# Score scale moved into the exponential, first pair's running sums added by small matmuls, row maxima written per head, and new engine, queue and order tables, in a fused attention and two-MLP kernel

## The chip, the cores and the metric

The kernel runs on one core of a Trainium2 chip. The metric is the device time of one execution in microseconds, the median over the runs; lower is better.

## The reference, cut to what matters

Three layers follow each other. The first is causal attention on 4 batches of 8 heads (32 heads, handled as 16 pairs) with 576 positions and head size 64, where each score gets a bias from running sums of `max(s, 0)`:

```python
scale = 1.0 / np.sqrt(D)
scores = scale * np.matmul(q, k.transpose(0, 1, 3, 2))
cum = np.cumsum(np.maximum(s, 0.0), axis=-1)
bias = -(cum[:, :, :, None] - cum[:, :, None, :])
scores = np.where(causal, -1000000000.0, scores + np.minimum(bias, 0.0))
attn = np.exp(scores - np.max(scores, axis=-1, keepdims=True))
attn = attn / (np.sum(attn, axis=-1, keepdims=True) + 1e-09)
out = np.matmul(attn, v)
```

The second layer is a gated MLP: `h = relu(x @ w_in)`, the second half of `h` is normalised over its features, mixed over positions by `w_spatial` (576 x 576) plus a bias, multiplied by the first half and projected by `w_out`. The third is `sigmoid(xr @ w_r) * (relu(xk @ w_k)**2 @ w_v)`, with `xk` and `xr` mixtures of a position and the one before. The MLP weights come in 64-bit floats.

## The kernel before, in words

**Tensors.** Every fp32 matrix product is made of fp32r matmuls on a high part and a low part of each operand, so a part is first copied ("high") and then subtracted ("low"). For a pair p of heads the tile `big` (three sets, set p % 3) holds four regions U, W, V, X. `st_T` (L347) fills them: `wh` and `xh` are the high parts of q and k, `ud` and `vd` copies of them on the other 64 partitions, `ul` and `vl` the low parts. A few of the first 64 rows of W and X are used as extra rows of the contraction: the three parts of the running sums (X rows 0 to 2, against ones in W) and the negated row maximum (W row 3).

**Stages of a pair.** `st_S` (L390) computes rough scores, high part by high part, in 12 units s0 to s11 (6 per head); each is one matmul (L397) into one of three PSUM buffers, and VectorE reduces it to row maxima (`jk`, L404). `fin` transposes the maxima (L416), ScalarE copies them (L418) and a DMA writes them into W row 3 (L419); one `fin` covers both heads, except for pair 0, which has one each (Ma, Mb). `st_E` (L431) computes the exact scores in units e0 to e9 with two matmuls per piece (L436), ScalarE takes the exponential (L457) and GpSimd zeroes above the diagonal (L461). `st_V` (L468) multiplies with v in blocks a0 to a4 and b0 to b4 (L480 to L484, plain fp32), `fa` and `fb` copy the result out (L494), and n1, n2, n2b, n30, n31 divide by the sums through two tiny DMAs and a broadcast DMA (`r`, `rd`, `rb`; L499, L506, L512, L516).

**Decoding.** In between, the weights are turned from 64-bit floats into high and low fp32r parts, in 64 jobs of 128 x 256: dL loads (L124), dF is two ScalarE instructions (L132, L133), dD three on VectorE and one on GpSimd (L138 to L145), dT a copy on ScalarE and a subtraction on GpSimd (L153, L154) into one of the buffers of `ring`, dS stores it (L158).

**Order.** The order of issue is written by hand, and each engine works in that order. `START` (L586) holds pair 0 and the first parts of pairs 1 and 2. `step(p)` for p = 1 to 14 runs, by the list `ORDER` (L527), the exact scores of pair p, the products with v of pair p-1, the rough scores of pair p+1 and the parts of pair p+2 (of which `vd` and `vl` come a step later). `TAIL1` and `TAIL2` (L857, L861) hold the end of attention, the fetch of the decoded weights WV and WU, the first products of the MLP (g0 to g4: 12 matmuls of 512 columns each; q0 to q7: 12 of 288), the statistics of g0 to g4 on VectorE and the preparation of `w_spatial` (p0 to p4). After them everything is ordered by loops. The table `ENGINE` (L111) says which engine makes a copy or subtraction, `QUEUE` (L114) which of the two hardware queues (SP or ScalarE's) issues a DMA.

**Pair 0.** The running sums of all heads are built in `aug` (32 partitions x 3 parts x 576, `sums`, `bases`, `sums2`, L315 to L327), which lies in set 2 of `big`. `rx00` and `rx01` (L330) are DMAs that put the rows of pair 0 into its X region; the first rough scores read them.

Of the kernel before, what the change touches and what calls it, by code (L numbers as in the profile page):

```python
# [25 lines left out]
def tile_kernel(  # L26
# [141 lines left out]
    def dec_part(nm):
        q, f, n = PARTS[nm]
        if len(q) <= (n if jobs else 0):  # L170
            return

        if nm == "dL" and len(loaded) + len(first) > 2:
            dec_part("dD" if first else "dF")
        if nm == "dF" and len(first) > 1:
            dec_part("dD")
        if nm == "dD" and len(second) > 1:
            dec_part("dT")
        if nm == "dT" and len(third) >= len(ring):
            dec_go("dS")  # L180
        if q:
            f(*q.pop(0))
# [122 lines left out]


# [40 lines left out]
    def st_T(p, pre="", heads=(slice(0, 2),)):  # L347
        g = p % G
        by = {"q": scale, "k": 1.0}

# [12 lines left out]
        def first(nm, i, eng):  # L363
            if eng == "S":
                nc.scalar.activation(out=hi(nm, i), in_=raw(nm, i), func=ACTF.Copy, scale=by[nm])
            else:
                (nc.gpsimd if eng == "P" else nc.vector).tensor_scalar(
                    out=hi(nm, i), in0=raw(nm, i), scalar1=by[nm], scalar2=1.0, op0=ALU.mult, op1=ALU.mult)

        def second(nm, i, eng):  # L370

            h = (hi if nm == "q" else dup)(nm, i).bitcast(F32)
            if eng == "P" and nm == "k":
                nc.gpsimd.tensor_tensor(out=lo(nm, i), in0=raw(nm, i), in1=h, op=ALU.subtract)
            else:
                nc.vector.scalar_tensor_tensor(  # L376
                    out=lo(nm, i), in0=raw(nm, i), scalar=by[nm], op0=ALU.mult, in1=h, op1=ALU.subtract)
# [12 lines left out]
    def st_S(p):  # L390
# [40 lines left out]
    def st_E(p):  # L431
# [154 lines left out]
    START = """cw0 ldk0 lds mask cx0 cx1 ldk1 sums bases sums2 ldq0 ldq1 0wh0 0wh1 0ul0 rx00 0ul1 rx01 augd 0xh1 dL dL  # L586
               pads1 0xh0 dL pads0 0ud0 s5 s0 0ud1 cw1 tiny s1 cw2 1wh1 ldq2 1wh0 s8 1ud0 s3 dF s10 dD 1ud1 dT lv1 s9
               0vd0 0vl0 cx2 s4 1rows dF 1ul1 s2 1ul0 Ma s6 ltv0 pads2 s7 1xh0 dS 1s0 2wh1 1xh1 1s4 dL dF 2wh0 dD dD
               1s10 s11 lv0 1s3 0vd1 e0 dT 0vl1 ldk2 1s6 e1 Mb 2ul0 2rows e3 2ud0 2xh1 2xh0 2ul1 1s2 1s1 1vd0 1vd1 ldq3
               2vd1 ldq4 1vl1 1s7 e2 e4 1s9 dS 1s8 2vl1 1s11 e5 e8 ones 1s5 e7 1M 1vl0 ldk3 2vd0 e9 2ud1 dL 2vl0 e6 dF"""  # L590
# [465 lines left out]
```

## Time and profile before

| | us |
|---|---|
| median of the runs (3) | 698.87 |
| lowest and highest run | 696.9, 701.27 |
| profiled execution, its own time | 697.19 |
| span of its profile, first to last instruction | 695.5 |

The profile is of one execution. Its span is cut into stretches in the rows below; each row of an engine's timeline has the start, the duration, the engine, the line, the operation, the tiles written and read, and in square brackets how long the engine had been idle and what ended that.

### The profile page before, as it was taken

Reading aid. Unit: us, or ns where it says so; the run is one execution under the profiler, and the core shown is the slowest. Engines: PE = TensorE matmul, PEld = TensorE weight load, DVE = VectorE, ACT = ScalarE, POOL = GpSimd, SP = SyncE. Lnnn points to the kernel's source line nnn. Section 1 sums busy time; section 2 is a strip of 40 time slices with the busy share of each in tenths; the row PEclk is TensorE's granted clock in tenths of the full one; section 3 lists DMA queues with packets and bytes.
Section 4 is the critical chain, followed back from the end, with each engine's and each line's share of the span. In section 5 each row is a group of like instructions: output and inputs, shape, how many; then the busy total and the mean of one; then the engine's idle time right before and its main releaser. Section 6 shows DMA issues by size and latency. Waiting matters only on the chain.

```text
span 695.5 us, 10926 instructions
## 1 busy us (share of the span) xinstructions
PE 655.0 (94%) x3657; PEld 562.8 (81%) x3657; DVE 520.1 (75%) x1053; ACT 357.5 (51%) x780; POOL 352.3 (51%) x497
## 2 busy tenths in 40 slices
PE   2699999999999859999999999999999999999998
PEld 1476766667767749999999999988989889898987
DVE  8969898989862487858868847269697786968763
ACT  4688888888763375565566453341323324133230
POOL 5655656665673346558458557242444444244330
PEclk9999999999999969999999999999999999999999
DMA  7455556564456626463254474440001010000101
GB/s 183 121 122 143 154 144 160 140 164 130 115 163 182 195 90 190 140 211 127 87 193 140 125 262 152 160 204 31 15 2 46 0 46 1 30 16 1 45 1 46
DMA packets 64880, 77.91 MB, mean 112 GB/s; under 512 B 28661, under 2 KB 45461, under 8 KB 64311
## 3 DMA queue, kind: packets, MB, share of 16 engines
q1 hardware_dynamic: 64433, 76.08, 36.6%
q10 hardware_dynamic: 390, 1.12, 0.6%
q8 instruction: 29, 0.48, 0.3%
q14 instruction: 28, 0.23, 0.1%
HBM read 54.05 MB, written 21.79 MB: 109 GB/s over the span
## 4 chain that ended last, share of the span: by engine, by line
PE 72%; DVE 13%; DMA 8%; ACT 2%; issue 2%; SPq 1%; POOL 1%; DVEq 0%; ACTq 0%; POOLq 0%
PE mm L682 54%; PE mm L767 7%; DVE jk L404 4%; PE ps L436 3%; DVE big L376 3%; DMA qk<-in_qk_dram 3%; PE pv L484 3%; PE s L397 2%; PE pv L481 1%; DMA d_wo<-hl 1%; DMA big<-d_wv 1%; DMA big<-mt 1%; DVE f L143 1%; DVE g L140 1%; DVE big L102 1%
## 5 line engine op out<-in xcount | busy, mean ns | idle before, releaser
L682 PE MATMUL mm<-big 128*128 128x384 f32 (+2 forms) x1176 | 203.4, 332 | 3.4 <-ACT vr L719 3.0
L682 PEld LDWEIGHTS mm<-big 128*128 128x128 f32 x1176 | 191.3, 188 | 12.9 <-ACT vr L719 3.4
L682 PE MATMUL mm<-w,vb 128*128 128x512 f32 (+1 forms) x304 | 90.4, 381 | 0.0
L965 DVE TENSOR_TENSOR r<-r 128x384 f32<-128x384 f32 x48 | 53.7, 1118 | 46.6 <-ACT r L962 46.6
L436 PE MATMUL ps<-big 128*128 128x288 f32 (+4 forms) x384 | 82.7, 334 | 4.3 <-DMA big<-mt 3.3
L397 PE MATMUL s<-big 128*128 128x288 f32 (+4 forms) x192 | 66.4, 416 | 16.9 <-DMA big<-big 12.3
L457 ACT ACTIVATE e<-ps 128x288 f32<-128x288 f32 (+3 forms) x160 | 64.0, 435 | 30.5 <-PE ps L436 28.5
L145 POOL TENSOR_TENSOR f<-f,raw 128x256 int32<-128x256 int32 x64 | 53.1, 829 | 45.6 <-DVE f L143 37.0
L397 PEld LDWEIGHTS s<-big 128*128 128x128 f32 x192 | 36.9, 205 | 46.2 <-DVE mx L404 21.8
L404 DVE CUSTOM_DVE_ANT_0 jk<-s,mask 64x64 bf16<-64x64 f32 (+4 forms) x160 | 64.4, 424 | 10.4 <-PE s L397 8.6
L436 PEld LDWEIGHTS ps<-big 128*128 128x128 f32 x384 | 60.7, 198 | 12.6 <-DMA big<-mt 4.6
L767 PE MATMUL mm<-ws,vb 128*128 128x288 f32 x384 | 60.5, 307 | 7.4 <-DVE ws L120 7.0
L682 PEld LDWEIGHTS mm<-w,vb 128*128 128x128 f32 x304 | 56.0, 188 | 11.2
L767 PEld LDWEIGHTS mm<-ws,vb 128*128 128x128 f32 x384 | 55.7, 197 | 8.8 <-DVE ws L120 8.1
L484 PE MATMUL pv<-e,vp 128*65 128x448 f32 (+2 forms) x192 | 62.6, 434 | 0.0
L120 POOL TENSOR_TENSOR hl<-f,hl 128x256 fp32r<-128x256 f32 x42 | 40.5, 965 | 42.5 <-ACT hl L105 42.3
L985 DVE RECIPROCAL rr<-rr 128x512 f32<-128x512 f32 x18 | 60.4, 3353 | 0.6
L461 POOL TENSOR_SCALAR_AFFINE_SELECT e<-e 128x128 f32<-128x128 f32 (+1 forms) x160 | 52.1, 357 | 14.9 <-ACT e L457 13.0
L966 ACT CAST vb<-r 128x384 fp32r<-128x384 f32 x48 | 24.6, 513 | 56.9 <-DVE r L965 56.9
L708 POOL TENSOR_TENSOR gh<-mix,vb 128x384 fp32r<-128x384 f32 x24 | 25.5, 1069 | 52.3 <-ACT vb L707 51.2
L682 PE MATMUL mm<-gh,wo 128*128 128x288 f32 x256 | 51.3, 294 | 0.0
L708 POOL TENSOR_TENSOR big<-mix,big 128x384 fp32r<-128x384 f32 x24 | 26.0, 1089 | 46.3 <-ACT big L707 37.6
(124 smaller groups left out, 1282.6 us busy)
## 6 DMA issues: line engine op xcount, KB each, us to landing
qk<-in_qk_dram SPq DMA_DIRECT2D x28, 288.0 KB
rb<-rd SPq DMA_DIRECT2D x16, 288.0 KB
out_dram<-rr SPq DMA_DIRECT2D x17, 256.0 KB
raw<-in_moe_w_in_dram SPq DMA_DIRECT2D x16, 256.0 KB
vp<-in_v_dram SPq DMA_DIRECT2D x16, 256.0 KB
raw<-in_moe_w_k_dram SPq DMA_DIRECT2D x16, 256.0 KB
raw<-in_moe_w_v_dram SPq DMA_DIRECT2D x16, 256.0 KB
big<-d_wk SPq DMA_DIRECT2D x8, 512.0 KB
```

The costliest lines, as they stand in the source:

```text
L145: nc.gpsimd.tensor_tensor(out=f, in0=f, in1=low, op=ALU.add)
L397: nc.tensor.matmul(out=ps[:, 0:kn], lhsT=W[g][:, h, 128 * i:128 * i + 128], rhs=X[g][:, h, k0:k0 + kn], start=True, stop=True,)
L404: nc.vector.tensor_tensor_reduce(out=jk[r0:128, 0:kn], in0=ps[r0:128, 0:kn], in1=mask[r0:128, m0:m0 + kn], scale=1.0, scalar=(dst if mid e ...
L436: nc.tensor.matmul(out=ps[:, o:o + b - a], lhsT=st[g][:, h, 128 * j:128 * j + 128], rhs=mv[g][:, h, 64 + a:64 + b], start=(n == 0), stop=( ...
L457: nc.scalar.activation(out=e[:, o:o + n], in_=ps[:, 0:n], func=ACTF.Exp)
L461: nc.gpsimd.affine_select(out=d, in_=d, pattern=[[1, w]], base=0, channel_multiplier=-1, compare_op=ALU.is_ge, fill=0.0,)
L484: nc.tensor.matmul(out=pv[0:VW, 1, 448 - w:448], lhsT=lt, rhs=e[:, OFF[j]:OFF[j] + w], start=False, stop=(j == 4),)
L682: nc.tensor.matmul(out=ps, lhsT=x, rhs=y, start=(m == 0), stop=(m == n - 1))
L708: nc.gpsimd.tensor_tensor(out=dst[1][:, kc, :], in0=t, in1=dst[0][:, kc, :].bitcast(F32), op=ALU.subtract)
L767: nc.tensor.matmul(out=o, lhsT=x[:, sc, dd], rhs=y[:, sc, t], start=(sc == 0 and m == 0), stop=False)
L965: nc.vector.tensor_tensor(out=r, in0=r, in1=r, op=ALU.mult)
L985: nc.vector.reciprocal(out=r, in_=r)
```

## The change

- The factor 1/8 on q goes: `wh` is a plain copy and `ul` a plain subtraction, so both can run on any engine. The running sums are multiplied by 8 instead (in the instruction that takes `max(s, 0)`), and the exponential gets `scale=1/8`.
- For pair 0 the rough scores no longer read the rows of the running sums in X: the contraction is over the 64 partitions of q and k alone, and three more matmuls per unit add the rows of `aug` through `pick`, a 32-row selection of a head (36 small matmuls in all).
- Ma and Mb, one per head, replace M for every pair.
- The rule by which a decode part first makes room moves from `dec_part` to `dec_go`.
- Two extra ring buffers are put in front of the ring instead of behind it, after TAIL1.
- `ENGINE`, `QUEUE`, `ORDER`, `START`, `TAIL1`, `TAIL2` are new. In the steps `ud` moves from ScalarE to GpSimd and `vd` from VectorE to ScalarE. For the last pairs the DMAs n13, d14, n15, d15 and b15 move from SP to ScalarE's queue.

```diff
+    pick = ec.tile([BH, 2, 128], F32R, name="pick")
...
+    def picks():
+        COPY[ENGINE["pk"]](pick, ident[0:BH, 0:2].rearrange("p (h o) -> p h o", o=1).broadcast_to([BH, 2, 128]))
...
-        nc.vector.tensor_scalar(out=srow, in0=srow, scalar1=0.0, scalar2=None, op0=ALU.max)
+        nc.vector.tensor_scalar(out=srow, in0=srow, scalar1=0.0, scalar2=1.0 / scale, op0=ALU.max, op1=ALU.mult)
...
+            COPY[eng](hi(nm, i), raw(nm, i))
...
+            subtract(eng, out=lo(nm, i), in0=raw(nm, i), in1=h)
...
+            lanes = slice(64, 128) if p == 0 else slice(0, 128)
             nc.tensor.matmul(
-                out=ps[:, 0:kn], lhsT=W[g][:, h, 128 * i:128 * i + 128], rhs=X[g][:, h, k0:k0 + kn],
-                start=True, stop=True,
+                out=ps[:, 0:kn], lhsT=W[g][lanes, h, 128 * i:128 * i + 128], rhs=X[g][lanes, h, k0:k0 + kn],
+                start=True, stop=p > 0,
             )
+            for r in range(3 if p == 0 else 0):
+                nc.tensor.matmul(
+                    out=ps[:, 0:kn], lhsT=pick[:, h, :], rhs=aug[:, r, k0:k0 + kn], start=False, stop=r == 2)
...
-        items.update({"Ma": lambda: fin(0, 1), "Mb": lambda: fin(1, 1)} if p == 0 else {"M": fin})
+        items.update({"Ma": lambda: fin(0, 1), "Mb": lambda: fin(1, 1)})
...
-            nc.scalar.activation(out=e[:, o:o + n], in_=ps[:, 0:n], func=ACTF.Exp)
+            nc.scalar.activation(out=e[:, o:o + n], in_=ps[:, 0:n], func=ACTF.Exp, scale=scale)
...
-    ORDER = """ltv s0 wh zero rows dT s4 lv a0 s1 s3 a1 ul n2 s6 xh n2b x1 vd s11 e0 e1 a2 s5 a3 dL a4 dD dS e3 fa e5
+    ORDER = """s4 wh s0 s3 zero a0 dT rows ltv s1 ul x1 n2 s6 xh lv a1 n2b e0 a2 e1 s5 a3 s11 dD vd x0 dL e2 s7 a4 s2
...
-    ring.extend(part_of(0, 4096 + 512 * i, 2, WN) for i in range(2))
+    ring[0:0] = [part_of(0, 4096 + 512 * i, 2, WN) for i in range(2)]
```

What the new tables make of three places is shown next. At the start, TensorE's first rows before, where each `L397` row is a unit of pair 0:

```order
L397 MATMUL s<-big 128x64
L397 MATMUL s<-big 128x288 x2
L397 MATMUL s<-big 128x448
L397 MATMUL s<-big 128x320
L397 MATMUL s<-big 128x192
```

and after, where `L394` is the product of q and k and `L399` the three parts of the running sums:

```order
L394 MATMUL s<-big 128x64
L399 MATMUL s<-big,pick 128x64 x3
L394 MATMUL s<-big 128x288
L399 MATMUL s<-big,pick 128x288 x3
L394 MATMUL s<-big 128x448
L399 MATMUL s<-big,pick 128x448 x3
```

Three matmuls stand behind each unit, and the unit's own one no longer reads the rows that a DMA brings. In a step, VectorE from the first subtraction (`ul`) on, before:

```order
L376 SCALAR_TENSOR_TENSOR big<-qk_134,big 64x2x576
L504 RECIPROCAL r_588<-r_588 128x9
L404 ISA jk,mx_141<-s,mask 128x288
L404 ISA mx_141 128x1
L102 CAST big<-big 64x2x576
L404 ISA jk,mx_141<-s,mask 64x64
L404 ISA mx_141 64x1
```

and after, in the same step:

```order
L120 TENSOR_TENSOR big<-qk_134,big 64x2x576
L504 RECIPROCAL r_634<-r_634 128x9
L404 ISA jk,mx_142<-s,mask 128x288
L404 ISA mx_142 128x1
L404 ISA jk,mx_142<-s,mask 64x64
L404 ISA mx_142 64x1
```

The copy `vd` (L102) has left VectorE's row; nothing stands in its place. In TAIL1, ScalarE from the last copy out of attention (`pt`, L494) on, before (`hl` are ring buffers, `vr` the ReLU of g2 and g3):

```order
L494 ACTIVATE pt_2821<-pv_2850,eps_139 65x576
L105 CAST hl0_85<-f_2867 128x256
L719 ACTIVATE vr_2892<-mm_2879 128x512
L719 ACTIVATE vr_2910<-mm_2897 128x512
L734 CAST vb_2693<-vr_2836 128x512
```

and after:

```order
L494 ACTIVATE pt_2935<-pv_2959,eps_139 65x576
L499 DMA r9_2986<-pt_2935 128x1x9
L720 ACTIVATE vr_3006<-mm_2993 128x512
L105 CAST hl0_85<-f_2975 128x256
L506 DMA rd_3015<-r9_2986 128x9
L720 ACTIVATE vr_3030<-mm_3017 128x512
```

The ReLU of g2 now stands ahead of the copy into `hl0`, and two DMAs of the last pair stand in ScalarE's row. SP's queue at the same place, before (`d_wu` to `big` is the fetch of WU):

```order
L499 DMA r9_2794<-pt_2730 128x1x9
L506 DMA rd_2842<-r9_2794 128x9
L203 DMA big_73<-d_wu_88 128x2x1024 x2
L512 DMA rb_2848<-rd_2842 64x1152
L124 DMA raw_2853<-in_moe_w_out_dram 128x256
L124 DMA raw_2855<-in_moe_w_out_dram 128x256
L499 DMA r9_2870<-pt_2821 128x1x9
L124 DMA raw_2872<-in_moe_w_out_dram 128x256
L158 DMA d_wo_89<-hl0_85 256x1x256
```

and after:

```order
L158 DMA d_wo_89<-hl0_85 256x1x256
L499 DMA r9_2921<-pt_2840 128x1x9
L124 DMA raw_2957<-in_moe_w_out_dram 128x256
L202 DMA big_73<-d_wu_88 128x2x1024 x2
L512 DMA rb_2971<-rd_2964 64x1152
L124 DMA raw_2978<-in_moe_w_out_dram 128x256
```

The store of `hl0`, which must land before the ring buffer is written again, moves from behind the fetch of WU and three loads to ahead of them, and the fetch no longer stands behind a wait for `r9`.

## Rows read from the trace of the kernel before

**Rows 1.** Stretches: start, length, busy us (count) PE PEld DVE ACT POOL, clock, DMA

```profile
12.30:33.00 20.70, 13.54 (x39) 9.62 (x39) 18.90 (x60) 12.38 (x26) 11.06 (x16) 1.00 0.56 136
134.52:146.09 11.57, 11.35 (x63) 8.05 (x61) 10.69 (x33) 9.89 (x20) 7.16 (x13) 1.00 0.58 152
210.50:234.20 23.70, 22.70 (x112) 17.70 (x112) 4.96 (x13) 5.97 (x13) 4.60 (x7) 1.00 0.75 226
234.20:258.30 24.10, 14.56 (x86) 12.53 (x86) 21.41 (x41) 17.25 (x39) 12.80 (x15) 0.82 0.26 78
258.30:274.00 15.70, 15.70 (x100) 15.70 (x101) 12.05 (x24) 8.33 (x21) 10.32 (x13) 0.84 0.51 146
274.00:695.50 421.50, 418.32 (x2412) 385.13 (x2411) 304.42 (x445) 164.67 (x391) 195.60 (x213) 1.00 0.26 90
```

**Rows 2.** The chain that ended last, at the start: start, us, what

```profile
7.70 4.49 DMA big<-big
12.32 0.81 PE s L397 x2
```

**Rows 3.** VectorE's timeline at the start

```profile
6.92 0.74 DVE L327 TENSOR_TENSOR big<-e,big 32x576 fp32r<-32x576 f32 x1
7.70 1.90 DVE L376 SCALAR_TENSOR_TENSOR big<-qk,big 64x576 fp32r<-64x576 f32 x2
9.62 1.40 DVE L367 TENSOR_SCALAR big<-qk 64x576 fp32r<-64x576 f32 x1
11.04 0.46 DVE L102 CAST big<-big 64x576 fp32r<-64x576 f32 x1
12.75 0.23 DVE L404 CUSTOM_DVE_ANT_0 jk<-s,mask 64x64 bf16<-64x64 f32 x1 [1.26 <-PE s L397]
```

**Rows 4.** TensorE's timeline: the transposes of the maxima, one in each step

```profile
47.48 0.27 PE L416 MATMUL s<-ident,mx 128*10 128x128 f32 x1
...
198.86 0.28 PE L416 MATMUL s<-ident,mx 128*10 128x128 f32 x1 [0.20 <-DVE mx L404]
```

**Rows 5.** VectorE's timeline in one step

```profile
134.52 0.76 DVE L102 CAST big<-big 64x1152 fp32r<-64x1152 f32 x1
...
143.17 0.52 DVE L404 CUSTOM_DVE_ANT_0 jk<-s,mask,mx 128x288 bf16<-128x288 f32 x1 [0.45 <-PE s L397]
...
146.09 0.76 DVE L102 CAST big<-big 64x1152 fp32r<-64x1152 f32 x1
```

**Rows 6.** Instructions of a line: count, ns shortest/median/longest, first and last start, forms

```profile
L516 DVE TENSOR_TENSOR x<-pt,rb x17: 745/753/1962, 59.4 to 244.1; 64x576 f32<-64x576 f32 x17
L108 POOL TENSOR_SCALAR big<-big x5: 669/1054/1261, 7.8 to 31.9; 64x576 fp32r<-64x576 f32 x5
```

**Rows 7.** Groups by line and form up to 195 us: busy us, mean ns

```profile
L516 DVE TENSOR_TENSOR x<-pt,rb 64x576 f32<-64x576 f32 x12 | 12.5, 1043 | 0.5 <-DMA rb<-rd 0.5
L418 ACT CAST mt<-s 10x128 fp32r<-10x128 f32 x14 | 3.3, 238 | 0.0
```

**Rows 8.** The chain that ended last, later: start, us, what

```profile
60.69 0.75 PE pv L481 x2
...
268.38 1.60 PE mm L767 x12
```

**Rows 9.** Waits over the whole span: engine, line, what for, us, times, longest

```profile
PE ps L436 <- DMA big<-mt: 3.3, 5, 1.2
```

**Rows 10.** SP's queue: the DMA of the maxima in a step, the fetch of WU

```profile
141.51 0.81 SPq L419 DMA_DIRECT2D big<-mt  x1
...
219.80 1.21 SPq L203 DMA_DIRECT2D big<-d_wu  x2
```

**Rows 11.** The chain that ended last, from 214 us

```profile
214.15 4.98 DMA r<-pt
...
224.71 9.07 DMA d_wo<-hl
```

**Rows 12.** ScalarE's timeline at the same place

```profile
221.86 0.74 ACT L494 ACTIVATE pt<-pv,eps 65x576 f32<-65x576 f32 x1 [0.79 <-PE pv L484]
233.86 0.41 ACT L105 CAST hl<-f 128x256 fp32r<-128x256 f32 x1 [11.26 <-DMA d_wo<-hl]
```

**Rows 13.** TensorE's timeline at the same place

```profile
216.12 3.01 PE L682 MATMUL mm<-big 128*128 128x512 f32 x12
...
221.63 11.61 PE L682 MATMUL mm<-big 128*128 128x512 f32 x60
```

**Rows 14.** VectorE's timeline: the statistics of g2

```profile
234.79 0.69 DVE L725 BATCH_NORM_STATS2 sv<-vr 128x6 f32<-128x512 f32 x1 [11.32 <-ACT vr L719]
```

More of the change, by code (lines that the diff above doesn't have):

```diff
@@ L164, in dec_go @@
     def dec_go(nm):
+        if nm == "dL":
+            while len(loaded) + len(first) > 2:
+                dec_go("dD" if first else "dF")
+        if nm == "dF" and len(first) > 1:
+            dec_go("dD")
+        if nm == "dD" and len(second) > 1:
+            dec_go("dT")
+        if nm == "dT" and len(third) >= len(ring):
+            dec_go("dS")
         q, f, _ = PARTS[nm]
@@ L168, in dec_part @@
     def dec_part(nm):
[L169 to L182, printed above, removed]
+        q, _, n = PARTS[nm]
+        if len(q) > (n if jobs else 0):
+            dec_go(nm)
     def dec_step():
@@ L348, in st_T @@
         g = p % G
-        by = {"q": scale, "k": 1.0}
         def raw(nm, i):
@@ L363, in first @@
         def first(nm, i, eng):
[L364 to L368, printed above, removed]
+            COPY[eng](hi(nm, i), raw(nm, i))
         def second(nm, i, eng):
             h = (hi if nm == "q" else dup)(nm, i).bitcast(F32)
[L373 to L377, printed above, removed]
+            subtract(eng, out=lo(nm, i), in0=raw(nm, i), in1=h)
         items = {"rows": lambda: prep_rows(p), "zero": lambda: no_max(p)}
@@ L526, in tile_kernel @@
     late = {}
-    ORDER = """ltv s0 wh zero rows dT s4 lv a0 s1 s3 a1 ul n2 s6 xh n2b x1 vd s11 e0 e1 a2 s5 a3 dL a4 dD dS e3 fa e5
-               e2 s10 n31 x0 s7 s2 ud x2 e4 b0 vl ldq s8 s9 e7 b1 ldk b2 x4 e6 n30 b3 b4 fb M e8 n1 x3 e9 dF""".split()
+    ORDER = """s4 wh s0 s3 zero a0 dT rows ltv s1 ul x1 n2 s6 xh lv a1 n2b e0 a2 e1 s5 a3 s11 dD vd x0 dL e2 s7 a4 s2
+               fa e3 ud s10 vl e5 e4 s8 dF b0 dS Ma e8 x2 s9 e7 b1 n31 b2 ldk b3 Mb n30 b4 x4 fb n1 e6 e9 ldq x3""".split()
     LATE = "vd vl"
@@ L575, in tile_kernel @@
         "pads0": lambda: pads(0), "pads1": lambda: pads(1), "pads2": lambda: pads(2), "tiny": tiny, "ones": ones,
-        "lds": load_s, "mask": masks,
+        "lds": load_s, "mask": masks, "pick": picks,
         "sums": sums, "sums2": sums2, "bases": bases,
@@ L585, in tile_kernel @@
                   for key in ("cw0", "cx0", "cw1", "cx1", "cw2", "cx2")})
[L586 to L590, printed above, removed]
+    START = """cx0 ldk0 mask cw0 lds cx1 pick sums ldq0 bases ldk1 sums2 ldq1 0wh0 0ul0 0wh1 dL augd rx00 0xh1 0ul1
+               pads1 dL rx01 0xh0 pads0 1wh1 0ud0 tiny 0ud1 cw1 s5 dL s0 ldq2 1wh0 1xh1 dF cx2 s8 s1 1ud0 s3 s10 0vd0
+               dD 1ud1 1rows s9 dT 0vl0 s4 1ul1 pads2 1xh0 s2 s6 1s0 dS dL ltv0 s7 1s4 1ul0 dF dD dF 0vd1 2rows s11 cw2
+               2wh1 2wh0 dD 2ud0 Ma 1s3 lv1 lv0 1s10 dT 0vl1 e0 1s6 e1 ldk2 Mb 2ul0 e3 2xh1 2ul1 1s2 1s1 1vd0 1vd1 2xh0
+               2vd1 1vl1 ldq3 e4 e2 ldq4 1s7 1s9 2vl1 1s11 1s5 e5 1s8 ones 2vd0 1vl0 1Ma e7 1Mb 2ud1 ldk3 dS e8 e9 dL
+               2vl0 dF e6"""
     for nm in START.split():
```

16 lines of the change are left out of this document (8 added, 8 removed).

## The prediction

> **What bounds the kernel now.** I read the stretches first [rows 1]. From 274 us to the end TensorE is busy 418.32 of 421.50 us; that part issues the same products and gains or loses nothing but through its start. What the change can move lies ahead of it, in four places, and in each the reader should ask which engine has no gap.
>
> At the start TensorE does nothing until 12.32 us; the chain shows why: a DMA from `big` to `big` (the rows of pair 0) of 4.49 us [rows 2]. VectorE, the busiest engine right behind (18.90 of 20.70 us [rows 1]), begins its first maximum at 12.75 us and had waited 1.26 us for it [rows 3].
>
> The steps have the period that the transposes mark: (198.86 - 47.48)/13 = 11.64 us [rows 4]. In one step, 11.57 us between two `vd` copies, VectorE waits once, 0.45 us, for TensorE [rows 5]. Its busy time is only 10.69 us [rows 1], but the rest is the few hundredths between its 33 instructions: VectorE is the bound. TensorE at 11.35 us is busy on paper, since its matmuls overlap; I work its need out below.
>
> From 210.50 to 234.20 us TensorE is busy 22.70 of 23.70 us, while VectorE does 4.96 us; from 234.20 to 258.30 us it is the other way, VectorE 21.41 of 24.10 us, TensorE 14.56 us at a mean granted clock of 0.82 [rows 1]. The reason is one wait: ScalarE, in order, stands at the copy into a ring buffer for 11.26 us, until the store of that buffer has landed [rows 12]; the store, issued late in SP's order, took 9.07 us [rows 11]. Behind the copy stand the ReLUs of g2 and g3, and VectorE's statistics of g2 wait 11.32 us, to 234.79 us [rows 14], although g2's matmuls were long done [rows 13].
>
> **The change part by part.** Durations come from the profiled execution, 697.19 us, which is 1.7 us under the median of the runs; sums are made against it.
>
> *Start.* The rough scores of pair 0 no longer wait for the DMA. They need `aug`, done at 6.92 + 0.74 = 7.66 us, and the high parts. What is late next is VectorE itself: ahead of its first maximum stand `ul0`, two copies and `ul1`, that is 1.90 us for the two subtractions and 2 x 0.46 for the copies [rows 3], with gaps 7.7 + 2.9 = 10.6 us. First maximum at 10.6 instead of 12.75: 2.1 us, and since VectorE is the bound up to the first step, it is carried on. The 36 small matmuls have 9600 columns; 12 matmuls of 288 columns take 1.60 us [rows 8], 0.46 ns a column, so 4.4 us of TensorE, which idles 7.2 of the 20.7 us there. That a matmul over 32 rows costs what its columns cost is not in the trace; half of it would change nothing. `pick` is one small GpSimd copy. Bounds: 0 (the fill now ahead of the k loads on ScalarE, or GpSimd, delays the first part), 3 us (also one fill fewer on VectorE). I take 2.1.
>
> *Steps.* `vd` leaves VectorE: 0.76 us and one gap of 0.03 [rows 5], 0.79 a step. The subtractions keep their operands and size, so their length. ScalarE gives `ud` and takes `vd`, the same form: no change, plus one more copy of maxima, 0.24 us [rows 7]: 9.89 to 10.13 of 11.57 us. GpSimd takes `ud`: 64 x 576 took it 0.67 to 1.26 us [rows 6], so 1.34 to 2.5 us for twice that, on 7.16 us: it has room. But a GpSimd instruction can stretch one of VectorE's with two operands in SBUF: the product L516, 0.745 us at best, reached 1.962 [rows 6] and had a mean of 1.043 [rows 7] with its twin on GpSimd beside it. `ud` comes in the order just ahead of `vl`, so I charge one such mean stretch, 0.30 us: 0.79 - 0.30 = 0.49, taken as 0.5 a step, 6.5 us over 13 periods. Is another engine late next? TensorE needs 9600 fp32r columns at 0.46 ns = 4.4 us and 3200 fp32 columns at 0.75/448 us [rows 8] = 5.4 us, with two transposes of some 0.1 us beyond their overlap about 10.0 us; ScalarE 10.13 plus gaps. So no more than 1.2 us a step can be won, 15.6 in all; the other bound is a full stretch of `vl` and `ul` (rival one).
>
> *Maxima for each head.* A second transpose, copy and DMA (0.81 us of SP's issue [rows 10]) in 15 pairs, hidden where SP idles between issues. Head 0's maxima are written half a step ahead of e0 instead of just before it: TensorE's 3.3 us of waits for that DMA [rows 9] go. Little of it lengthened a period: I take 0.6, between 0 and 3.3. VectorE and the `fin` buffers share the three PSUM buffers of the rough scores; the second `fin` takes one for a short while.
>
> *Exponential with a scale, sums times 8, `dec_go`.* No instruction is added; cost taken as 0, between -0.5 and 0.5 us.
>
> *Tail.* The store of `hl0` now goes out ahead of the fetch of WU, and the next two copies after the first go to buffers from `big`, so the 11.26 us wait should go; SP no longer holds the fetch of WU, issued at 219.80 us [rows 10], behind a wait for `r9`. The ReLU of g2 stands ahead of the copy. g1's 12 matmuls took 3.01 us [rows 13] with their latency, some 2.73 each in a row, so g2 ends near 221.63 + 2.7 + 0.3 = 224.6, g3 near 227.4 and g4 near 230 us. VectorE's chain of 258.3 - 234.8 = 23.5 us could start at 225: 9.8 us is the most. Late next is ScalarE's new wait: it issues `r`, `rd` and `rb` of the last pair itself, and stands at `rd` until `r` has landed. Behind it are the ReLU of g3 and the copies. `r` of the pair before took 4.98 us, the store 9.07 [rows 11]. Issued at 222.6, `r` lands at 227.6 or 231.7; then g3's statistics come at about 228.5 or 232.5 instead of 236. I take a gain of 6 us (by the 4.98 us row, as `r` is as small), between 2 and 9.8. SP also waits at `rb` for `rd`, with two loads behind it, which feed decoding only. VectorE's decodes ahead of the first spatial product fall by one (some 1.2 us), which I leave as reserve.
>
> The Trainium skill, DMA: Bandwidth & Descriptors, "Issuing engines are not separate DMA queues", says that DMAs of all issuers run on the same 16 engines and another issuer only saves issue time. By that rule the three tiny DMAs gain nothing in transfer from ScalarE's queue; the trace agrees as far as it goes, `r` taking 4.98 us there beside bulk traffic [rows 11]. The sum would stay 6 by the short row and fall to about 2 by the long one.
>
> Sum: 697.2 - 2.1 - 6.5 - 0.6 - 6.0 = 682.0 us.
>
> **The rivals.** *One, slower: GpSimd's `ud` holds VectorE up for its whole length.* In each step `vl`, `ul` or a product of n30 waits for all of `ud`, up to 2.5 us, so a period grows by 2.5 - 0.79 = 1.7 us, 22 over 13, against 8.7 won elsewhere: 697.2 + 22 - 8.7 = 710.5. It decides from a stretch of 0.79 + 8.7/13 = 1.5 us a step. For: the longest L516, stretched by 1.22 us [rows 6]. Against: its mean stretch, 0.30 [rows 7], and most of VectorE's work in a step are maxima, with one operand in PSUM.
>
> The Trainium skill, SBUF — State Buffer, "SBUF: two separate sides", calls the port pair of VectorE and GpSimd an exclusive lock, held for a whole instruction against a VectorE instruction with two SBUF inputs. By that rule a collision costs up to the whole `ud`, which is rival one if it happens in every step; the 1.962 us row agrees with it, the mean of 1.043 says that it is seldom full.
>
> *Two: the wait on ScalarE only changes its cause.* The `rd` wait lasts as the store did, 9.07 us, and the blocked SP queue holds loads back; the tail gains nothing: 697.2 - 9.2 = 688.0. For: bulk traffic fills this stretch (DMA share 0.75 [rows 1]). Against: g2's ReLU is ahead of it.
>
> *Three: another engine takes over the steps.* TensorE, held by the few buffers, or ScalarE keeps the period at 11.6: 697.2 - 8.7 = 688.5. For: both need over 10 us of it. Against: 1.2 us of room.
>
> *Four: two and three together,* the change then does little of what it says: 697.2 - 2.7 = 694.5.
>
> **How the numbers follow.** Forecast 0.55, two 0.17, three 0.13, four 0.08, one 0.07. A measurement here tells about 1% (7 us) from no change: below 691.9 is faster, which the forecast and rivals two and three are (0.85; I keep 0.83 for the spread of the runs); four is the same (0.10 with that spread); one is slower (0.07). The range: the terms at their high ends (3, 15.6, 3.3 and 9.8) would reach 665.5, which I don't expect together; with the start and the tail at their best and 0.8 a step it is 697.2 - 3 - 10.4 - 0.6 - 9.8 = 673.4, and I go to 673. Above, it takes in rivals two and three and stops at 691.
>
> **What would show it.** Right: VectorE's first maximum near 10.6 us; transposes of one head's maxima about 11.1 us apart; no wait of TensorE for `mt`; no 11 us wait of ScalarE, the statistics of g2 within 2 us of its matmuls, and the stretch before the first spatial product shorter by about 6 us at a higher clock. Wrong: periods still of 11.5 us or more with `vl` over 2 us, a long wait of ScalarE at `rd` or a decode load, or a longer stretch after 274 us, where the fetch of `w_out` must land before the projections.

## The result and the profile after

The changed kernel takes 690.99 us (median of 4 runs, 689.8 to 691.2), the kernel before 700.07 us in the same comparison (4 runs, 696.9 to 702.61): a ratio of 0.987 with a 95% interval of 0.982 to 0.991. The profiled execution took 691.16 us with a span of 689.4 us. The forecast was 682.0 us. Between the two profiled spans 6.1 us are gained, where the sum of the prediction had 15.2.

Where they went is read from four marks that both timelines have: the last transpose of the maxima of pair 1, of pair 2 and of pair 15, and the first product behind the spatial ones of batch 0.

| us | before | after | difference | predicted |
|---|---|---|---|---|
| start, to the transpose of pair 1 | 34.66 | 40.39 | +5.7 | -2.1 |
| first step | 12.82 | 13.60 | +0.8 | 0 |
| 13 periods of the steps | 151.38 | 148.52 | -2.9 | -7.1 |
| tail, to 273.82 and 267.69 | 74.96 | 65.18 | -9.8 | -6.0 |
| from there to the end | 421.7 | 421.7 | 0 | 0 |

The marks that [rows 4] doesn't have, before:

```profile
34.66 0.41 PE L416 MATMUL s<-ident,mx 128*10 128x128 f32 x1
...
273.82 1.52 PE L682 MATMUL mm<-big 128*128 128x512 f32 x6
```

and after:

```profile
40.39 0.41 PE L416 MATMUL s<-ident,mx 128*5 128x128 f32 x1
...
53.99 0.27 PE L416 MATMUL s<-ident,mx 128*5 128x128 f32 x1
...
202.51 0.27 PE L416 MATMUL s<-ident,mx 128*5 128x128 f32 x1
...
267.69 7.68 PE L683 MATMUL mm<-big 128*128 128x512 f32 x33
```

So the start lost where it should have gained, the steps gave less than half of what was forecast, and the tail gave more. Stretches of the kernel after (columns as in [rows 1]): the start, one step, and the stretch that held the 11 us wait:

```profile
8.00:28.00 20.00, 19.84 (x51) 12.93 (x52) 11.66 (x39) 8.77 (x17) 6.55 (x12) 1.00 0.53 125
137.80:149.10 11.30, 11.04 (x64) 8.03 (x63) 9.94 (x32) 9.86 (x21) 8.90 (x15) 1.00 0.58 152
210.00:240.00 30.00, 29.68 (x156) 23.42 (x156) 15.31 (x36) 12.62 (x28) 12.79 (x21) 1.00 0.71 232
```

In all three TensorE is the engine with the smallest gaps (0.16, 0.26 and 0.32 us). VectorE, which the prediction took for the bound of the first two places, is busy 11.66 of 20.00 us at the start and 9.94 of 11.30 us in a step.

**The start.** TensorE's timeline, a unit of 288 columns and the start of the next one:

```profile
8.46 0.60 PE L394 MATMUL s<-big 64*128 64x288 f32 x1
9.00 1.08 PE L399 MATMUL s<-big,pick 32*128 32x288 f32 x3
10.01 0.74 PE L394 MATMUL s<-big 64*128 64x448 f32 x1
```

and the group of all small matmuls up to 28 us (busy us, mean ns):

```profile
L399 PE MATMUL s<-big,pick 32*128 32x288 f32 (+4 forms) x36 | 13.4, 497 | 0.3 <-DVE big L332 0.3
```

VectorE's first maximum comes at 10.46 us, as forecast (10.6). But a unit takes TensorE 1.55 us, and VectorE waits for nine of the twelve, 7.9 us in all. The waits that are new or longer (columns as in [rows 9]):

```profile
DVE jk L404 <- PE s L399: 7.9, 9, 1.1
PEld ps L436 <- ACT e L457: 10.3, 26, 1.0
```

**A step.** The copy `vd` on ScalarE, the exponential e2 behind it, and TensorE, which waits for a buffer that e2 reads:

```profile
139.47 1.15 ACT L105 CAST big<-big 64x1152 fp32r<-64x1152 f32 x1
140.53 0.53 ACT L457 ACTIVATE e<-ps 128x448 f32<-128x448 f32 x1
...
141.12 0.63 PE L436 MATMUL ps<-big 128*128 128x192 f32 x4 [0.26 <-ACT e L457]
```

**The tail.** SP's queue and ScalarE, where the fetch of WU now goes out at 218.74 us and the ReLU of g2 waits only for its products:

```profile
218.74 4.59 SPq L202 DMA_DIRECT2D big<-d_wu  x2
...
227.81 0.60 ACT L720 ACTIVATE vr<-mm 128x512 f32<-128x512 f32 x1 [2.02 <-PE mm L683]
```

The 11.26 us of [rows 12] are gone. The chain (columns as in [rows 11]) shows the last pair's sums, which land in 3.85 us:

```profile
225.82 3.85 DMA r<-pt
```

### The profile page after: what moved, and what is told of

Same layout as the page of the kernel before. It is cut to its first block, busy times and chain, and to the rows that moved or that the text cites. A ratio compares the mean times of both kernels' runs of the same rounds, so it can differ in the third digit from the quotient of the medians.

```text
span 689.4 us, 11164 instructions
## 1 busy us (share of the span) xinstructions
PE 666.0 (97%) x3708; PEld 570.5 (83%) x3708; DVE 510.2 (74%) x1038; ACT 359.1 (52%) x795; POOL 373.7 (54%) x512
## 4 chain that ended last, share of the span: by engine, by line
PE 86%; DVE 6%; DMA 4%; ACT 2%; issue 1%; SPq 0%; POOL 0%; ACTq 0%; DVEq 0%
PE mm L683 55%; PE mm L768 7%; PE ps L436 6%; PE pv L484 6%; PE s L394 4%; PE pv L481 3%; DMA r<-pt 2%; PE s L399 2%; DVE big L120 1%; DVE jk L404 1%; PE pv L480 1%; ACT e L457 1%; DMA vt<-in_v_rest_dram 1%; PE mm L769 1%; PE mm L770 1%
## 5 line engine op out<-in xcount | busy, mean ns | idle before, releaser
L436 PE MATMUL ps<-big 128*128 128x288 f32 (+4 forms) x384 | 91.4, 347 | 5.0 <-ACT e L457 2.9
L436 PEld LDWEIGHTS ps<-big 128*128 128x128 f32 x384 | 61.5, 199 | 23.8 <-ACT e L457 10.3
L404 DVE CUSTOM_DVE_ANT_0 jk<-s,mask 64x64 bf16<-64x64 f32 (+4 forms) x160 | 62.5, 424 | 18.9 <-PE s L394 11.3
L394 PE MATMUL s<-big 128*128 128x192 f32 (+6 forms) x192 | 64.5, 379 | 9.5 <-POOL big L282 6.8
L457 ACT ACTIVATE e<-ps 128x288 f32<-128x288 f32 (+3 forms) x160 | 62.5, 430 | 9.5 <-PE ps L436 6.7
L768 PE MATMUL mm<-ws,vb 128*128 128x288 f32 x384 | 58.9, 302 | 4.1 <-DVE ws L120 4.1
L394 PEld LDWEIGHTS s<-big 128*128 128x128 f32 (+1 forms) x192 | 37.1, 205 | 24.3 <-issue 9.5
L120 POOL TENSOR_TENSOR hl<-f,hl 128x256 fp32r<-128x256 f32 x41 | 44.1, 1074 | 20.0 <-ACT hl L105 19.1
L461 POOL TENSOR_SCALAR_AFFINE_SELECT e<-e 128x128 f32<-128x128 f32 (+1 forms) x160 | 46.5, 314 | 10.8 <-ACT e L457 8.6
```

The costliest lines, as they stand in the source:

```text
L120: (nc.gpsimd if eng == "P" else nc.vector).tensor_tensor(op=ALU.subtract, **kw)
L394: nc.tensor.matmul(out=ps[:, 0:kn], lhsT=W[g][lanes, h, 128 * i:128 * i + 128], rhs=X[g][lanes, h, k0:k0 + kn], start=True, stop=p > 0,)
L404: nc.vector.tensor_tensor_reduce(out=jk[r0:128, 0:kn], in0=ps[r0:128, 0:kn], in1=mask[r0:128, m0:m0 + kn], scale=1.0, scalar=(dst if mid e ...
L436: nc.tensor.matmul(out=ps[:, o:o + b - a], lhsT=st[g][:, h, 128 * j:128 * j + 128], rhs=mv[g][:, h, 64 + a:64 + b], start=(n == 0), stop=( ...
L768: nc.tensor.matmul(out=o, lhsT=x[:, sc, dd], rhs=y[:, sc, t], start=(sc == 0 and m == 0), stop=False)
```

## The experiments

All times are medians beside the kernel before on the same chip, with the ratio to it. Marks are those of the table above.

**1. The small matmuls undone.** Every unit of pair 0 again reads the rows in X:

```diff
-lanes = slice(64, 128) if p == 0 else slice(0, 128)
+lanes = slice(0, 128)
...
-for r in range(3 if p == 0 else 0):
+for r in range(0):
```

> The changed kernel, but the rough scores of pair 0 are again made by one matmul over all 128 partitions that reads the rows in X, and the 36 small matmuls are gone. Theory A (TensorE, whose small matmuls took 0.34 to 0.47 us each, holds the start): the first maximum comes at about 12.8 us instead of 10.5, but the transposes of pair 1 at about 34.5 us instead of 39.5, so the time falls by 5 to 6 us to about 685. Rival B (the new order of START and the fills hold VectorE, the small matmuls only fill its gaps): the transposes stay at 39 us or later and the time is 690 to 693.

684.9 us (683.9 to 688.14), ratio 0.980 [0.975, 0.984]. The first maximum came at 12.72 us and the transpose of pair 1 at 34.19 instead of 40.39. Theory A holds, rival B falls: the part that was to win 2.1 us at the start costs 6.2 there.

**2. Nine of the 36 kept.** Only the first three units use them:

```diff
+few = p == 0 and (h, i, k0) in ((0, 0, 0), (0, 4, 0), (1, 3, 0))
+lanes = slice(64, 128) if few else slice(0, 128)
```

> The changed kernel, but only the first three units of pair 0 add the running sums by small matmuls (9 of the 36); the other nine read the rows in X, which have landed by about 12.5 us. Theory A: the first maximum stays at 10.5 us and the units after it cost TensorE 0.5 us instead of 1.6, so the start gains both the 2 us that the change was meant to give and the 5.7 us that it lost: transposes of pair 1 at about 32.5 us, the time about 684. Rival B: transposes at 39 us, 690 to 693.

683.55 us (682.88 to 684.93), ratio 0.977 [0.972, 0.981], the fastest kernel of the study. VectorE's start and the transpose of pair 1 (here the lines of the units are one higher):

```profile
12.21 2.63 PE L395 MATMUL s<-big 128*128 128x288 f32 x6
...
12.19 0.62 DVE L405 CUSTOM_DVE_ANT_0 jk<-s,mask 128x448 bf16<-128x448 f32 x1 [1.00 <-PE s L400]
19.00 0.46 DVE L405 CUSTOM_DVE_ANT_0 jk<-s,mask 128x288 bf16<-128x288 f32 x1 [0.99 <-PE s L395]
...
34.32 0.41 PE L417 MATMUL s<-ident,mx 128*5 128x128 f32 x1
```

VectorE is the bound again. Still the mark stands at 34.32 us, not at the 32.5 expected: 0.3 us better than before. In this kernel an earlier first maximum alone is worth little. Its time cannot be told from the one of experiment 1 by these intervals.

**3. TensorE kept busy ahead of the small matmuls.**

```diff
+nc.vector.memset(X1[0:128, 3, 3, 1:S + 1], 0.0)
+hot = ps_v.tile([128, 2, 512], F32, tag="pv", name="pv")
+for _ in range(4):
+    nc.tensor.matmul(out=hot[:, 0, :], lhsT=X1[0:128, 3, 3, 1:129], rhs=X1[0:128, 3, 3, 1:513], start=True, stop=True)
```

> The changed kernel with all 36 small matmuls, plus four plain fp32 matmuls of 128x128 by 128x512 on zeros ahead of everything on TensorE, which is idle there until 6.8 us; their result is not read. Theory A1 (the small matmuls are dear because the loads and matmuls of the first 40 us run at the slow level, 0.28 us a load against 0.19 later, although the profile prints a granted clock of 1.00): behind the four, loads take 0.19 us and a unit of 288 columns about 0.7 us instead of 1.55, VectorE no longer waits for them, transposes of pair 1 at about 32.5 us, the time about 684. Rival A2 (the price lies in the form, 32 rows of weights or the rows of the moving tile, at any level): units still take 1.5 us, and the time is 691, or up to 1 us more because the four end late.

688.64 us (686.31 to 691.08), ratio 0.984 [0.980, 0.988]. TensorE's timeline:

```profile
1.61 6.67 PE L595 MATMUL pv<-x 128*128 128x512 f32 x8 [1.61 <-DVE x L592]
...
8.88 0.40 PE L394 MATMUL s<-big 64*128 64x288 f32 x1
9.21 0.67 PE L399 MATMUL s<-big,pick 32*128 32x288 f32 x3
...
11.01 0.60 PE L394 MATMUL s<-big 64*128 64x288 f32 x1
11.54 1.08 PE L399 MATMUL s<-big,pick 32*128 32x288 f32 x3
```

and its stretches (the clock is the third number from the end):

```profile
8.20:11.00 2.80, 2.80 (x13) 1.87 (x12) 2.65 (x8) 0.00 (x0) 0.00 (x0) 1.00 1.05 242
11.00:20.00 9.00, 9.00 (x24) 6.13 (x24) 4.73 (x18) 5.38 (x11) 4.94 (x9) 0.50 0.63 127
```

Half of theory A1 is shown: behind the four products (eight records) the same unit takes 0.40 + 0.67 instead of 0.60 + 1.08 us, at a granted clock of 1.00 (2.4 GHz). But after 11 us, with only the units of pair 0 (products over 32 and 64 rows) between and no gap, the rows are as long as in the changed kernel, and now the column says 0.50, the 1.2 GHz level. So three units were quick, and the mark moved by 1.1 us to 39.30. Rival A2 has a share too: even at the fast level such a unit is 0.93 us from start to start, against VectorE's 0.5 for its maximum.

**4. `vd` moved into ScalarE's idle time.**

```diff
-LATE = "vd vl"
+LATE = "vl"
...
-a3 s11 dD vd x0 dL
+a3 s11 dD x0 dL
...
-b3 Mb n30 b4
+b3 vd Mb n30 b4
```

> The changed kernel, but in the steps the copy vd stands on ScalarE in the 1.2 us in which it waits for the second transpose of the maxima, and so belongs to the pair two steps on; nothing of its length changes. Theory C (in the steps TensorE waits 0.3 to 0.5 us for the exponential that stands behind vd): the wait of TensorE for the exponential (10.3 us in all, 26 times) falls by half or more, and the period of the steps from 11.29 to about 11.0 us, 3 to 4 us in all, the time about 687.5. Rival D (TensorE's own 11.04 us of work per step is the bound, whatever the order): period 11.2 to 11.3, the time 690 to 692. Rival E (the copy in the gap delays the maxima row or the last exponentials): slower, 693 or more.

695.74 us (694.16 to 696.75), ratio 0.994 [0.992, 0.996]; the 13 periods took 154.33 us, 11.87 each: rival E by the time. Theory C's first half came true: TensorE's wait for the exponential (the 10.3 us above) fell to 1.4 us. But it waits 14.2 us instead of 6.2 for VectorE's maxima, and the trace has a cause that none of the three had. `vl` on VectorE and `ud` on GpSimd:

```profile
145.11 2.34 DVE L120 TENSOR_TENSOR big<-qk,big 64x1152 fp32r<-64x1152 f32 x1
...
145.09 1.16 POOL L108 TENSOR_SCALAR big<-big 64x1152 fp32r<-64x1152 f32 x1
```

The copy began 0.02 us ahead, and the subtraction took its own 1.35 us and about 1.0 more, in 12 of the 13 steps. In the changed kernel it is mostly the other way round, and once as here:

```profile
96.67 2.34 DVE L120 TENSOR_TENSOR big<-qk,big 64x1152 fp32r<-64x1152 f32 x1
...
142.34 1.37 DVE L120 TENSOR_TENSOR big<-qk,big 64x1152 fp32r<-64x1152 f32 x1
...
142.60 2.14 POOL L108 TENSOR_SCALAR big<-big 64x1152 fp32r<-64x1152 f32 x1
```

Whichever starts first runs at its own length, the other waits it out. This is what the Trainium skill, SBUF — State Buffer, "SBUF: two separate sides", says of the port pair of the two engines (an exclusive lock, held for a whole instruction); the trace agrees, with 1.35 or 2.34 us and 1.15 or 2.14 us and little between in the steps of this kernel and of the changed one. Eight of the profiled kernels have the same code in the steps, and differ in how often VectorE lost:

| kernel | 2 | changed | 1 | 3 | 7 | 8 | 11 | 10 |
|---|---|---|---|---|---|---|---|---|
| `vl` of 2.3 us, of 13 | 0 | 1 | 1 | 1 | 2 | 4 | 4 | 5 |
| 13 periods, us | 147.43 | 148.52 | 148.66 | 148.52 | 149.19 | 150.91 | 150.93 | 152.05 |

Between the last and the first of them a loss costs (152.05 - 147.43)/5 = 0.9 us. The 12 losses of experiment 4 cost less, 154.33 - 147.43 = 6.9 us, while TensorE's wait for the exponential went away.

What goes ahead of a loss is in the traces too. In 17 of the 18 losses of the table, VectorE's reciprocal of the sums in the same step had waited 0.34 to 0.70 us for its DMA, as here in the changed kernel, 3.5 us ahead of the `vl` at 96.67 us:

```profile
93.13 0.22 DVE L504 RECIPROCAL r<-r 128x9 f32<-128x9 f32 x1 [0.49 <-DMA r<-pt]
```

In the steps without a loss that wait was at most 0.27 us, but for one of 0.36 us. `vl` then comes so late that `ud` is 0.01 to 0.03 us ahead of it. In the 18th loss (experiment 1) VectorE had waited 0.46 us at a decode.

**5. The same, with `ud` earlier.**

```diff
-a3 s11 dD x0 dL e2 s7 a4 s2 fa e3 ud s10 vl
+a3 s11 ud dD x0 dL e2 s7 a4 s2 fa e3 s10 vl
```

> The kernel with vd in the 1.2 us gap, in which the subtraction vl on VectorE and the copy ud on GpSimd began within 0.03 us of each other in every step and vl took 2.34 us instead of 1.35, with ud moved ahead of the decoding sum, into GpSimd's 1.4 us of idle time, beside VectorE's maxima. Theory F (two instructions with SBUF operands on VectorE and GpSimd exclude each other, the later one waits for the whole of the earlier one, and this alone made the kernel with vd in the gap slower): vl 1.35 us and ud 1.15 us in each step, no wait of TensorE for the maxima of the last units, period 11.8 us down to 11.1 to 11.3, the time 686 to 691. Rival G (the gap itself is the harm: the maxima's copy and the last exponentials stand behind vd): vl falls to 1.35, but the period stays above 11.5 and the time above 693.

699.44 us (698.52 to 700.69), ratio 0.999 [0.998, 1.001], 12.13 us a period. The first half of theory F came true (`vl` 1.40 us in every step), the second did not:

```profile
130.80 0.21 DVE L504 RECIPROCAL r<-r 128x9 f32<-128x9 f32 x1
...
131.79 1.21 DVE L138 TENSOR_SCALAR g<-g 128x256 f32<-128x256 f32 x1
...
143.46 0.22 DVE L504 RECIPROCAL r<-r 128x9 f32<-128x9 f32 x1 [0.48 <-DMA r<-pt]
...
143.90 1.16 POOL L108 TENSOR_SCALAR big<-big 64x1152 fp32r<-64x1152 f32 x1
144.45 0.76 DVE L138 TENSOR_SCALAR g<-g 128x256 f32<-128x256 f32 x1
...
146.66 0.47 PE L394 MATMUL s<-big 128*128 128x448 f32 x1 [0.80 <-DVE mx L404]
```

`ud` now begins just ahead of a decode on VectorE (0.29 us elsewhere) and holds that up instead of `vl`, in every step of the 13 periods that has a `ud`. At 144.45 us the decode takes 0.47 us more, behind a wait of 0.48 us for the DMA of the sums; a step earlier, without that wait, it takes 0.92 us more. So VectorE comes about 0.9 us late either way, ahead of a maximum whose PSUM buffer TensorE waits for, 0.80 us here and 1.25 in the step before. The period and the time are where rival G put them, but its cause isn't shown: the collision that theory F names was moved and not removed, and no kernel has `vd` in the gap without one.

**6. The engines of before in the new order.**

```diff
-wh="S", xh="S", ud="P", vd="S", ul="V", vl="V"
+wh="S", xh="S", ud="S", vd="V", ul="V", vl="V"
```

> The changed kernel with the engines of before in the steps: vd on VectorE again, ud on ScalarE, everything else and the order as changed. Theory H (the engine table made the gain of the steps): the period goes back to 11.5 to 11.7 us, the time to 694 to 696. Rival I (the gain came from the order and from the maxima for each head): the period stays at 11.3 to 11.4, the time at 690 to 692.

699.66 us (698.69 to 701.27), ratio 1.000 [0.998, 1.002]: theory H, and more than it expected.

```profile
144.88 0.76 DVE L102 CAST big<-big 64x1152 fp32r<-64x1152 f32 x1
...
146.25 0.47 PE L394 MATMUL s<-big 128*128 128x448 f32 x1 [1.13 <-DVE mx L404]
```

VectorE's `vd` stands ahead of the maximum, TensorE waits 1.13 us, and a period is 12.04 us, longer than before the change. `ud` went back together with `vd`; which of the two does it was not tried.

**7. Ring buffers behind the ring.**

```diff
-ring[0:0] = [part_of(0, 4096 + 512 * i, 2, WN) for i in range(2)]
+ring.extend(part_of(0, 4096 + 512 * i, 2, WN) for i in range(2))
```

> The changed kernel with the two extra ring buffers behind the ring again, so that the first two copies after the first spatial preparations go to the two old buffers. Theory J (which buffer comes first decides the tail): ScalarE waits 3 us or more for a store again, the statistics or the parts of the spatial weights come later, the time 693 to 698. Rival K (the store of the first buffer now goes out early, and the ReLUs stand ahead of the copies, so the ring's order no longer matters): wait under 1 us, the time 690 to 692.

691.47 us (690.91 to 692.68), ratio 0.988 [0.984, 0.992]. In this kernel a decoded part of `w_out` is overwritten before its store is issued (the new rule counts the four buffers, not the stores still open), so that part is changed, and the copy has no store to wait for. It doesn't test theory J; experiment 11 does.

**8. The five DMAs of the last pairs on SP's queue.** n13, d14, n15, d15 and b15 go from "A" to "P" in `QUEUE`.

> The changed kernel with the five tiny DMAs of the last pairs on SP's queue again, at the same places of the order. Theory L (SP's queue, which stands still at each of them until its producer is done, holds back the fetch of WU and the loads, and so the MLP's first products): the fetch of WU goes out 1 us or more later, the tail grows by 2 us or more, the time 693 or more. Rival M (moving them gained only the issue time): 690 to 692. Rival N (on ScalarE they hold the ReLUs back, so that SP is better): below 689.

700.85 us (698.7 to 703.42), ratio 1.001 [0.999, 1.004]. Of the 12.3 us between the spans 2.4 lie in the steps (four losses of `vl`), 9.95 in the tail, which takes 75.13 us, as before the change. SP's queue, and VectorE behind it:

```profile
227.30 0.34 SPq L506 DMA_DIRECT2D rd<-r  x1
228.09 1.96 SPq L202 DMA_DIRECT2D big<-d_wu  x2
...
232.23 0.57 SPq L499 DMA_DIRECT2D r<-pt  x1
...
242.17 0.22 DVE L504 RECIPROCAL r<-r 128x9 f32<-128x9 f32 x1 [11.16 <-DMA r<-pt]
```

Theory L: the fetch of WU stands behind `rd` and goes out 23.2 us behind the last transpose of the maxima instead of 16.2. Then the last pair's `r`, issued at 232.23 us behind it, takes 9.93 us to land instead of 3.85, and g2's statistics stand behind VectorE's reciprocal. ScalarE's wait of 11.26 us for the store is gone here too, and this wait of 11.16 us on VectorE stands in its place: with the queue of before, the new order of the tail and of the ring gains nothing (75.13 against 74.96 us).

**9. The old order with the new engines.** In the kernel before, `ud` on GpSimd and `vd` on ScalarE, nothing else.

> The kernel before with nothing changed but the engines of two copies in the steps: ud from ScalarE to GpSimd, vd from VectorE to ScalarE. Theory P (VectorE bounds the steps of before, and its 0.79 us per step are the gain whatever the order): the period falls from 11.64 us to about 11.2, the time by 5 to 6 us, to about 694. Rival Q (the table is worth something only together with the new order, because in the old one ScalarE's vd or GpSimd's ud, stretched to 2.1 us beside vl, stands ahead of what TensorE waits for): the period stays at 11.5 us or grows, the time within 2 us of 699 or above.

702.2 us (700.93 to 706.35), ratio 1.005 [1.003, 1.008]: rival Q. A period is 12.15 us.

```profile
140.45 1.15 ACT L105 CAST big<-big 64x1152 fp32r<-64x1152 f32 x1
141.51 1.01 ACT L457 ACTIVATE e<-ps 128x288 f32<-128x288 f32 x3
...
141.96 0.96 PE L436 MATMUL ps<-big 128*128 128x288 f32 x4 [1.27 <-ACT e L457]
```

In the old order `vd` on ScalarE stands behind three other copies and ahead of three exponentials, and TensorE waits 1.27 us a step.

**10. One of the five alone.** d14 goes back to "P".

> The changed kernel with one of the five DMAs of the last pairs back on SP's queue: the 1152 reciprocals of pair 14 (d14), which then stand ahead of the fetch of WU. Theory R (this one wait of SP delays the fetch by some 8 us, and its 4 MB then lie ahead of the last pair's tiny DMAs): the fetch goes out at about 227 us instead of 218.7, the last pair's sums take 8 us or more to land instead of 3.85, and the tail grows by most of the 9.8 us that all five cost: 697 to 701. Rival S (the last pair's three DMAs on ScalarE's queue are what helps): 690 to 693.

696.14 us (692.66 to 697.14), ratio 0.995 [0.993, 0.997]. The tail took 68.88 us, 3.7 more than the changed kernel's; in the steps the profiled execution had five losses of `vl` and took 3.5 us more. SP's queue:

```profile
225.38 1.49 SPq L202 DMA_DIRECT2D big<-d_wu  x2
```

and the chain:

```profile
228.54 7.42 DMA r<-pt
```

Theory R has the mechanism but only 3.7 of the 9.95 us. The fetch (2 MB in two DMAs, not the 4 MB of the expectation) goes out 20.5 us behind the last transpose and `r` takes 7.42 us, though ScalarE's queue issues it; the other 6.2 us come only with the other four DMAs on SP as well. Theory and rival share it.

**11. Ring behind, open stores first.**

```diff
+while third:
+    dec_go("dS")
+ring.extend(part_of(0, 4096 + 512 * i, 2, WN) for i in range(2))
```

> The changed kernel with the two extra ring buffers behind the ring, and the stores that are still to be issued then issued first, so that the next two copies on ScalarE do wait for the stores of the two old buffers. Theory J: ScalarE waits 2 us or more for a store, and the first spatial product comes later, the time 693 to 698. Rival K (the order of the ring no longer matters, since the first store goes out early): 690 to 692.

693.61 us (692.23 to 694.04), ratio 0.991 [0.988, 0.994]. ScalarE's wait for a store, at 242.22 us, is 0.16 us, and the tail 65.55 us (changed kernel 65.18): rival K in the tail. The time itself fits theory J's range, but for another reason, four losses of `vl` in the steps.

**12. `vd` behind e2, with nine small matmuls.**

```diff
-s11 dD vd x0 dL e2 s7
+s11 dD x0 dL e2 vd s7
```

> The kernel with nine small matmuls (measured at 683.55 us), with vd behind the exponential e2 on ScalarE instead of ahead of it. Theory C (TensorE waits once in each step, 0.26 us, for that exponential): the wait goes and the period falls from 11.30 to 11.1 us or less, 2 to 3 us in all, to about 681. Rival D2 (fa and the three exponentials behind it come 0.25 us later and TensorE waits there instead): no change, 683 to 684.5.

688.24 us (687.39 to 688.69), ratio 0.983 [0.978, 0.988], 4.7 us slower than experiment 2, which neither theory had. `ud` and `vl` no longer meet (1.15 and 1.35 us), and TensorE's wait for e2 at that place is gone. But `fa` is late, as rival D2 said, and TensorE waits there (0.24 us) and for a maximum (0.32 us); the period is 11.66 us.

```profile
136.63 0.47 PE L395 MATMUL s<-big 128*128 128x448 f32 x1 [0.32 <-DVE mx L405]
137.34 0.43 PE L481 MATMUL pv<-e,vp 128*65 128x128 f32 x2 [0.24 <-ACT pt L495]
```

## Why the prediction was right or wrong

The direction held. The size did not: 9.1 us between the medians, 6.1 between the profiled spans, of 15.2. That the range held is luck: 690.99 us lies 0.01 us inside its upper end, and only because errors of opposite sign were added up, 7.8 us at the start, 0.8 in the first step and 4.2 in the periods against 3.8 the other way in the tail.

*Start: wrong, by 7.8 us.* The step that failed is "12 matmuls of 288 columns take 1.60 us, 0.46 ns a column, so 4.4 us of TensorE". That row [rows 8] is from 268 us, at the fast level. The 36 small matmuls took 13.4 us, and with the twelve products of q and k they filled TensorE from 8 to 27 us. A row of the same place stood in the prediction: two matmuls with together 352 columns took 0.81 us [rows 2], where 0.46 ns a column would make it 0.16. By that price three small matmuls of 288 columns take 0.40 us; they took 1.08 us, and 0.67 us where experiment 3 had TensorE at the fast level, so the level is the larger part of the error and not the whole. Experiments 1 and 2 show the term: without them, or with nine, the mark goes from 40.4 to 34.2 or 34.3 us. The second half of the step, that 2.1 us of head start "is carried on", fell too: with nine small matmuls the first maximum was 2.3 us earlier and the mark 0.3 us. VectorE waited 2.0 us for two units in between.

*Steps: right direction, less than half the size.* Two errors. First, "ScalarE 10.13 plus gaps" and TensorE's need of "about 10.0 us", leaving 1.2 us a step. The row said 11.35 us busy [rows 1], and it was argued away; now TensorE is busy 11.04 of 11.30 us, and the rest is its wait for e2 behind `vd`. In experiment 6, where steps of 12.22 and 12.01 us leave it room, TensorE is still busy 11.09 and 10.90 us. So by these runs its need was sized 1 us too low, and the room was 0.3 and not 1.2 us. Rival three (another engine takes over) came true for the part beyond 0.3 us a step. Second, the lock was charged as a mean of 0.30 us in each step; in the kernels of the new order and engines it is all or nothing, 1.0 us in 0 to 5 of 13 steps, and moves the total by up to 4.6 us from one kernel to another with the same steps. Experiments 6 and 9 show that the 0.5 us of `vd` belong to engines (of `vd` and `ud`, moved together) and order (with the maxima per head) together:

| mean period, us | engines of before | new engines |
|---|---|---|
| order of before | 11.64 | 12.15 |
| new order | 12.04 | 11.34 to 11.70 |

Either one alone is slower than neither. A price for `vd` "off VectorE" does not exist by itself; what counts is which instruction TensorE waits for stands behind it, on either engine.

*Maxima per head.* TensorE's waits for that DMA in the steps are gone, as forecast (one of 1.9 us stands at the start instead). What that was worth was not tried by itself.

*Tail: right, at its upper bound.* The 9.8 us are "the most" that was named, and the choice of 6 was too careful. Of the edits named, the ring's order is worth 0.4 us (experiment 11) and the queue of five tiny DMAs 9.95, with the new order in place (experiment 8). The prediction had the queue as half a sentence ("SP no longer holds the fetch of WU ... behind a wait for `r9`"). It decides whether `r` lands in 4 us or in 10, the two rows between which the term was chosen. The new order took the 11.26 us wait away, as the prediction said, but without the queue a wait as long came in its place. Whether the queue alone would gain anything in the old order, where ScalarE stood still for the store, was not run, so how the two share the 9.8 us stays open. The rule that the prediction cites from the Trainium skill (DMA: Bandwidth & Descriptors, "Issuing engines are not separate DMA queues"), that another issuer saves only issue time, is not contradicted for the transfer itself: from ScalarE's queue too `r` took 3.85 us in the changed kernel and 7.42 us in experiment 10. But the row that the prediction set beside it, 4.98 us, is of a DMA on SP's queue, and what a waiting DMA holds back on its queue was left out. Rival two did not come: the wait at `rd` was short. In experiment 10 it did, with 5.17 us on ScalarE ahead of a ReLU.

*Rival one* (the lock makes it slower) did not decide the changed kernel, but its mechanism is real. It stood in 12 of 13 steps of experiment 4, 4.7 us slower than the changed kernel, and on the decode in experiment 5; how much of the 4.7 us is its doing was not separated.

What stays open: why the DMA of the sums comes late in some steps and in some kernels with the same code, and with it the losses of `vl`; and the first step, 0.8 us longer than before in the profile, which experiments 1 and 8 show as well (13.6 us) and four of the other kernels with the same steps don't (12.5 to 12.6 us).

## What to carry to other kernels

Take a duration from the same stretch of the trace in which the new instruction will run; a row from 268 us made the small matmuls of the first 28 us three times too cheap (4.4 against 13.4 us). Before moving work off the busiest engine, name the instruction behind it on the engine that receives it, and who waits for that: either half of a move by itself can be slower than none. Where two engines exclude each other, moving one instruction can move the collision to another pair (experiment 5), so look at what will run beside it. A DMA that waits for data should not stand ahead of a big fetch on the same queue, however small it is.

## What the runs showed of the hardware that was not expected

The clock column is no guide at the start of these traces. In the changed kernel it reads 1.00 from 8 to 28 us, with the same durations (0.60 and 1.08 us a unit) that experiment 3 prints at 0.50. The weight loads tell it, 0.28 us against 0.19 us; in the changed kernel they switch only here:

```profile
44.36 0.28 PEld L394 LDWEIGHTS s<-big 128*128 128x128 f32 x1 [0.51 <-DVE mx L404]
44.83 0.19 PEld L394 LDWEIGHTS s<-big 128*128 128x128 f32 x1 [0.19 <-issue]
```

Before that TensorE had worked without a long gap from 37.85 us, on products over 128 rows; in the kernel before the loads switch at 38.34 us, behind such work from 32.2 us. From 8 to 28 us TensorE was busy 19.84 of 20.00 us, mostly on products over 32 and 64 rows, and the loads stayed at 0.28 us or more; in experiment 3 such products alone stood between the stretch at 1.00 and the fall to 0.50 at 11 us. Why the level stayed low in the one and fell in the other was not separated.
